# Two-stage agent attention with a routed expert: factors no longer normalised ahead of the split, and an explicit instruction order

## The chip, the cores and the metric

The kernel runs on one core of one Trainium2 chip. The metric is the device time of one execution in microseconds (us). The engines are PE (TensorE, matmuls; PEld is its weight load), DVE (VectorE), ACT (ScalarE), POOL (GpSimd) and SP (SyncE, which here issues nearly all DMA transfers).

## What is computed

For 4 batches of 12608 tokens with 128 channels and 49 agents, attention goes in two steps, and then a small expert corrects the 128 best tokens of each batch:

```python
def sm(a, b):
    s = scale * (a @ b.transpose(0, 2, 1))
    s = s - s.max(-1, keepdims=True)
    e = np.exp(s)
    return e / (e.sum(-1, keepdims=True) + 1e-09)
a2k = sm(agents, k)          # 49 x 12608
agent_v = a2k @ v            # 49 x 128
q2a = sm(q, agents)          # 12608 x 49
x = q2a @ agent_v
# expert: per batch, the 128 tokens with the largest x @ w_gate
h = np.maximum(x[top] @ w1, 0.0)
out[top] = x[top] + sigmoid(score[top])[:, None] * (h @ w2)
```

## The kernel before

**Tiling.** A batch is 99 columns of 128 tokens, in seven chunks: six of 15 columns (long, 960 KB a load) and chunk 6 of 9 (short, 576 KB). (b, c) is batch b, chunk c. k, q and v are loaded by chunk; tiles of loads and of finished outputs share the ring "inp" of 6 buffers (N_IN), and the batch-0 outputs that fill gaps (FILL) have a ring "og" of 2.

**The k side.** `scores` (k_front) multiplies a chunk with the agents on PE: tile S, in two halves, from a PSUM ring of 3. DVE transposes each half into sk and takes its maximum into mx. When all seven chunks are there, k_max makes the maxima of the batch (mT and mB on PE, then mb on DVE). k_exp subtracts mb on POOL and exponentiates on ACT. v_tiles multiplies with v on PE (av), and v_finish (pw and pp on PE, then DVE and ACT) makes ws, the values in two f16 parts, and iv, a power of two.

**The q side.** q_scores makes sq in the same way, with a maximum per token qm on DVE. q_exp subtracts qm on POOL and exponentiates on ACT; for batches in EARLY (0 and 1) DVE then sums, ACT adds a small constant, DVE takes the reciprocal, and q_high multiplies the factors with it on POOL. q_high copies the factors to f16 (ACT); q_low subtracts on POOL to get the low part; both stand in f. q_turn transposes f on PE (fT), ACT or DVE copies it to ft. q_gate makes gate scores and sums on PE (pg). q_rates, once all seven gates of a batch are there, makes the scores of the batch and, for batches not in EARLY, r, the reciprocal sum per token. topk (all, gt, pc and the rest) finds the 128 tokens.

**Outputs.** q_out multiplies ft and ws on PE, four columns at a time (po); an eviction writes og. MODES names the engine of each group of four: V is DVE, A is ACT, P is ACT with a POOL multiplication behind it. For EARLY batches the eviction scales with iv alone, for others with r (in V by DVE, in P by POOL). A chunk that is complete is stored by SP. At the end expert gathers the tokens (xq), multiplies (qT, sc, eT, xT, xe, ph, py on PE), and scatters its result once the stores of its batches have landed.

**The order.** All this is first recorded as a list of steps (Recorder; a step is one instruction or one group of matmuls), in program order and with dependencies. `place` then plays a model of the engines, with the priorities of the table RANKS, and returns the order in which the steps are issued; each engine works its part of it in order. PE has 452 steps in it, SP 118.

Of the kernel before, what the change touches and what calls it, by code (L numbers as in the profile page):

```python
# [40 lines left out]
EARLY = (0, 1)  # L41
MODES = ('AVAV', 'AVAV', 'VPVP', 'VPVP')
# [6 lines left out]
SLACK = 0.0  # L49
STICK = 10922.517314977244  # L50
# [202 lines left out]
HALF = ("po", "fT", "pg")  # L253
WINDOW, STAY, RISE = 3413.333, 0.45, 0.76
WORK = {"S": 1.0, "av": 0.89, "po": 0.93, "pg": 0.25, "fT": 0.8, "all": 0.83, "ph": 0.9}
RATE, GATHER, SCATTER = 408.0, 6500.0, 2400.0


def switch(a, b):

    if a in HALF and b in HALF:
        return 10.0
    return 160.0 if a == "av" else 100.0 if a == "S" or b in ("S", "av") else 50.0


def lag(a, b):

    if a.engine == b.engine:
        return 0.0 if a.engine == "PE" else a.tail
    return a.tail + 70.0  # L270


class Clock:


    def __init__(self):
        self.window, self.did, self.full = 0, 0.0, False

    def cost(self, op, t):
        while t >= (self.window + 1) * WINDOW:  # L280
            self.full = self.did >= (STAY if self.full else RISE) * WINDOW
            self.window, self.did = self.window + 1, 0.0
        few = op.kind == "pg"
        c = op.cost * (1.0 if self.full or few else 2.0)
        over = max(0.0, t + c - (self.window + 1) * WINDOW)
        self.did += (c - over) * WORK.get(op.kind, 0.5)
        if over:
            self.full = self.did >= (STAY if self.full else RISE) * WINDOW
            self.window, self.did = self.window + 1, over * WORK.get(op.kind, 0.5)
        return c  # L290


def place(rec, urgency, slack=0.0, stick=0.0):

    ops = rec.ops
    users, takes = {}, [[] for _ in ops]
    for op in ops:
        for name in sorted(op.uses):
            if name not in users:
                takes[op.seq].append(rec.rings[name][0])  # L300
            users.setdefault(name, []).append(op)
    rank = [(urgency(op.tag, op.engine), op.seq) for op in ops]
    room = {ring: bufs for ring, bufs in rec.rings.values()}
    left = {name: len(u) for name, u in users.items()}
    after = [[] for _ in ops]
    missing = [len(op.deps) for op in ops]
    for op in ops:
        for d in op.deps:
            after[d].append(op)
    ready = [0.0] * len(ops)  # L310
    queue = {e: [op for op in ops if op.engine == e and not op.deps] for e in ENGINES.values()}
    free = dict.fromkeys(queue, 0.0)
    last = dict.fromkeys(queue, "")
    times, ends, order = [0.0], [], []
    line, clock = 0.0, Clock()
    while len(order) < len(ops) or ends:
        if not times:
            raise RuntimeError("no instruction can begin")
        now = heapq.heappop(times)
        while ends and ends[0][0] <= now + 1e-6:  # L320
            op = ops[heapq.heappop(ends)[1]]
            for x in after[op.seq]:
                more = slack if x.engine == "PE" and op.engine != "PE" else 0.0
                ready[x.seq] = max(ready[x.seq], op.end + lag(op, x) + more)
                missing[x.seq] -= 1
                if not missing[x.seq]:
                    queue[x.engine].append(x)
                    heapq.heappush(times, ready[x.seq])
            for name in op.uses:
                left[name] -= 1  # L330
                if not left[name]:
                    room[rec.rings[name][0]] += 1
        for e, waiting in queue.items():
            if free[e] > now + 1e-6:
                continue
            best = None
            for op in waiting:
                if ready[op.seq] > now + 1e-6:
                    continue
                key = rank[op.seq]  # L340
                if op.kind == last[e]:
                    key = (key[0] - stick, key[1])
                if best is not None and key >= best[0]:
                    continue
                need = takes[op.seq]
                if all(room[r] >= need.count(r) for r in need):
                    best = (key, op)
            if best is None:
                continue
            op = best[1]  # L350
            waiting.remove(op)
            order.append(op)
            for r in takes[op.seq]:
                room[r] -= 1
            op.start = max(now, free["POOL"]) if op.two else now
            cost = op.cost
            if e == "PE":
                if last[e] != op.kind:
                    op.start += switch(last[e], op.kind) if last[e] else 50.0
                cost = clock.cost(op, op.start)  # L360
            last[e] = op.kind
            free[e] = op.end = op.start + cost
            if op.kind == "dma_start":
                line = max(line, op.start + 1800.0) + op.size / RATE
                op.end = line + 1700.0
            elif op.size:
                op.end += GATHER if op.label.startswith("xq") else SCATTER
            heapq.heappush(ends, (op.end, op.seq))
            heapq.heappush(times, op.end)
            heapq.heappush(times, free[e])  # L370
    return sorted(order, key=lambda op: (op.start, op.seq))


RANKS = {
    ('setup', 0): {"ACT": -7704.603, "POOL": -40854.573, "DVE": -34695.979},
# [9 lines left out]
    ('kmax', 0): {"DVE": 41091.545, "PE": 58712.794},  # L385
    ('exp', 0, 0): {"POOL": -88028.326, "ACT": 169482.5},
    ('exp', 0, 1): {"POOL": -22401.104, "ACT": 321716.736},
    ('exp', 0, 2): {"POOL": 70975.178, "ACT": 315931.785},
    ('exp', 0, 3): {"POOL": 58294.679, "ACT": 304754.866},
    ('exp', 0, 4): {"POOL": 39134.622, "ACT": 334237.156},  # L390
    ('exp', 0, 5): {"POOL": 51140.999, "ACT": 225861.786},
    ('exp', 0, 6): {"POOL": 55847.904, "ACT": 305110.098},
    ('v', 0, 0): {"SP": 11990.05},
    ('av', 0, 0): {"PE": 42293.51},
    ('v', 0, 1): {"SP": 20852.403},
    ('av', 0, 1): {"PE": -95203.721},
    ('v', 0, 2): {"SP": 25732.307},
    ('av', 0, 2): {"PE": 48113.417},
    ('v', 0, 3): {"SP": 26879.58},
    ('av', 0, 3): {"PE": 36554.066},  # L400
    ('v', 0, 4): {"SP": -154.989},
    ('av', 0, 4): {"PE": -244316.769},
    ('v', 0, 5): {"SP": 27655.575},
    ('av', 0, 5): {"PE": 87914.589},
    ('v', 0, 6): {"SP": 28400.238},
    ('av', 0, 6): {"PE": 38896.804},
    ('fin', 0): {"DVE": -136605.102, "PE": -175038.306, "POOL": 41207.367, "ACT": 135592.531},
    ('q', 0, 0): {"SP": -22705.261, "PE": 83217.232, "DVE": 73912.386},
    ('qe', 0, 0): {"POOL": 74676.234, "ACT": 353340.888, "DVE": 25400.62},
    ('turn', 0, 0): {"PE": 110425.037, "DVE": 86067.107, "ACT": 171382.578},  # L410
    ('gate', 0, 0): {"PE": 26353.217},
    ('q', 0, 1): {"SP": -23034.369, "PE": 53477.308, "DVE": -145606.484},
    ('qe', 0, 1): {"POOL": 82352.64, "ACT": 322967.816, "DVE": 37860.525},
    ('turn', 0, 1): {"PE": 83936.752, "DVE": 87178.494, "ACT": 316575.984},
# [228 lines left out]
    ('expert', 2): {"POOL": 38822.733, "PE": 214325.217, "DVE": -26426.609, "ACT": 335914.832},  # L643
    ('expert', 3): {"POOL": -240553.185, "PE": 107739.067, "DVE": -50621.084, "ACT": 308149.546},
}


def urgency(tag, engine):

# [864 lines left out]
```

## Time and profile before

| | us |
|---|---|
| median of 3 runs | 289.97 (289.36 to 291.24) |
| the profiled execution | 289.3 |
| its span | 287.4 |
| PE busy | 266.9 |
| DVE busy | 224.3 |
| POOL busy | 183.4 |
| ACT busy | 171.6 |
| moved by DMA | 106.68 MB |

Busy time is the time in which an engine executes something; matmuls are pipelined and their ends are modelled. A timeline row gives start and duration of merged instructions of one kind, with the idle time ahead of them and what ended it in brackets. A piece of the chain of waits lasts until the next piece of the chain begins. The granted clock of PE is given as a share of full speed.

### The profile page before, as it was taken

To read this page: it belongs to the slowest core of one execution; us is meant where nothing else is said; L and a number is where in the kernel's file an instruction comes from. 1 tells how busy PE (TensorE), PEld (TensorE's weight loads), DVE (VectorE), ACT (ScalarE), POOL (GpSimd) and SP (SyncE) were. 2 spreads that over 40 slices of the span, in tenths; PEclk is the share of its full clock that TensorE was granted. 3 is DMA by queue.
4 is the path that set the end of the run, shared out by engine and by line. 5 is a ranking of instruction groups with operands and counts; after the bars stand their busy time and mean duration, and the time that the engine had idled before them with its cause. 6 is when DMAs were issued, how large, how long until landed. Compare 5 with 4: busy or idle time off the path is not lost.

```text
span 287.4 us, 8559 instructions
## 1 busy us (share of the span) xinstructions
PE 266.9 (93%) x3524; PEld 176.3 (61%) x3524; DVE 224.3 (78%) x517; ACT 171.6 (60%) x313; POOL 183.4 (64%) x152
## 2 busy tenths in 40 slices
PE   1985798999999999999999999999999999999992
PEld 0221235594557645536455974656798789898992
DVE  1897897977999888997788979558925869998730
ACT  1004156553168965518496988979979854975500
POOL 8014799894189999119998329998422234784723
PEclk9999799999999999999999999889999999999997
DMA  7999999999999999999999999999813585999981
GB/s 281 424 408 419 422 426 415 422 417 422 418 421 391 380 423 410 408 421 412 418 423 419 421 422 414 413 420 373 320 52 148 222 349 220 414 413 408 419 372 48
DMA packets 18203, 106.68 MB, mean 371 GB/s; under 512 B 2032, under 2 KB 3440, under 8 KB 18160
## 3 DMA queue, kind: packets, MB, share of 16 engines
q1 hardware_dynamic: 17760, 105.42, 90.1%
q8 instruction: 30, 0.49, 0.7%
q0 software_dynamic: 256, 0.52, 0.5%
q10 hardware_dynamic: 144, 0.13, 0.1%
q14 instruction: 13, 0.11, 0.1%
HBM read 79.85 MB, written 26.21 MB: 369 GB/s over the span
## 4 chain that ended last, share of the span: by engine, by line
PE 65%; POOL 12%; DMA 9%; ACT 7%; DVE 3%; issue 3%; POOLq 0%; ACTq 0%
PE S L1435 24%; PE av L1435 13%; PE po L1435 13%; PE fT L1435 6%; POOL sk L1435 5%; DMA xT<-kT 4%; DMA out<-og 3%; POOL f L1435 3%; PE pg L1435 2%; PE all L1435 2%; ACT gt L1435 2%; PE ph L1435 2%; POOL sq L1435 2%; DMA ag_sb<-agT 2%; ACT ft L1435 2%
## 5 line engine op out<-in xcount | busy, mean ns | idle before, releaser
L1435 PE MATMUL S<-xT,ag_sb 128*32 128x480 f32 (+1 forms) x896 | 102.4, 572 | 10.8 <-DMA ag_sb<-agT 6.0
L1435 POOL TENSOR_TENSOR sq<-sq,qm 128x735 f32<-128x735 f32 (+1 forms) x42 | 56.9, 1368 | 34.9 <-DVE qm L1435 27.8
L1435 PEld LDWEIGHTS <-ft 128*128 128x128 f16 x1188 | 59.1, 98 | 15.1 <-issue 13.3
L1435 POOL TENSOR_TENSOR f<-sq,f 128x735 f16<-128x735 f32 (+1 forms) x28 | 42.7, 1527 | 23.5 <-ACT f L1435 21.2
L1435 PEld LDWEIGHTS S<-xT,ag_sb 128*32 128x32 f32 x896 | 23.5, 111 | 54.1 <-issue 24.6
L1435 PE MATMUL po<-ws,ft 128*128 128x128 f16 x792 | 53.5, 220 | 0.5 <-ACT og L1435 0.4
L1435 POOL TENSOR_TENSOR sk<-sk,mb 128x735 f32<-128x735 f32 (+1 forms) x28 | 47.2, 1703 | 8.8 <-DVE mb L1435 8.8
L1435 PE MATMUL av<-v,sk 128*64 128x129 f32 x792 | 49.9, 275 | 0.4 <-DMA v<-va 0.4
L1435 PEld LDWEIGHTS av<-v,sk 128*64 128x64 f32 x792 | 44.5, 136 | 8.5 <-DMA v<-va 3.6
L1435 ACT COPY ft<-fT 128x896 f16<-128x896 f16 (+2 forms) x49 | 43.7, 896 | 8.8 <-PE fT L1435 8.6
L1435 DVE STREAM_TRANSPOSE sq<-S 128x480 f32<-128x480 f32 (+1 forms) x56 | 35.5, 639 | 11.6 <-POOL f L1435 8.4
L1435 DVE STREAM_TRANSPOSE sk<-S 128x480 f32<-128x480 f32 (+1 forms) x56 | 35.1, 635 | 6.3 <-PE S L1435 3.5
L1435 DVE TENSOR_REDUCE qm<-sq 128x15 f32<-128x735 f32 (+1 forms) x42 | 36.1, 865 | 1.2 <-ACT sq L1435 0.7
L1435 ACT ACTIVATE sq<-sq,lift 128x735 f32<-128x735 f32 (+1 forms) x28 | 25.0, 891 | 19.5 <-POOL sq L1435 19.3
L1435 DVE TENSOR_REDUCE mx<-S 128x1 f32<-128x480 f32 (+1 forms) x56 | 33.0, 607 | 3.1 <-PE S L1435 2.9
L1435 POOL TENSOR_TENSOR og<-og,r 128x512 f32<-128x512 f32 (+1 forms) x26 | 24.3, 944 | 14.1 <-ACT og L1435 13.9
L1435 PEld LDWEIGHTS <-f 128*128 128x128 f16 x396 | 22.9, 98 | 12.2 <-issue 7.6
L1435 ACT ACTIVATE sk<-sk 128x735 f32<-128x735 f32 (+1 forms) x28 | 22.4, 799 | 12.4 <-POOL sk L1435 12.2
L1435 PE MATMUL fT<-idh,f 128*128 128x128 f16 x396 | 28.8, 220 | 0.8 <-POOL f L1435 0.8
L1435 ACT CAST f<-sq 128x735 f16<-128x735 f32 (+1 forms) x28 | 22.2, 793 | 11.1 <-POOL sq L1435 10.5
L1435 ACT ACTIVATE og<-po,iv 128x512 f32<-128x512 f32 (+1 forms) x28 | 18.0, 663 | 12.6 <-PE po L1435 11.5
L1435 DVE SCALAR_TENSOR_TENSOR gt<-all,top,minus 128x512 bf16<-128x512 f32 x32 | 23.6, 739 | 0.9 <-PE all L1435 0.5
(131 smaller groups left out, 251.2 us busy)
## 6 DMA issues: line engine op xcount, KB each, us to landing
v<-va SPq DMA_DIRECT2D x24, 967.5 KB, 8.8
xT<-kT SPq DMA_DIRECT2D x24, 960.0 KB, 9.1
xT<-qT SPq DMA_DIRECT2D x24, 960.0 KB, 9.0
out<-og SPq DMA_DIRECT2D x24, 960.0 KB, 6.4
v<-va SPq DMA_DIRECT2D x4, 580.5 KB, 6.9
xT<-kT SPq DMA_DIRECT2D x4, 576.0 KB, 8.8
xT<-qT SPq DMA_DIRECT2D x4, 576.0 KB, 9.1
out<-og SPq DMA_DIRECT2D x4, 576.0 KB, 5.6
```

The costliest lines, as they stand in the source:

```text
L1435: call(*args, **kwargs)
```

## The change

EARLY becomes empty, so no batch has its factors summed and scaled in q_exp and q_high; all four batches get r in q_rates, and all outputs are evicted in the modes V and P with r. The planner with its model, its prices and RANKS goes; `place` returns the steps in the order of a list of numbers, ORDER, each number being a step's place in the recorded program. The copies into f get their dependency on the two clearing memsets by name.

```diff
-EARLY = (0, 1)
-MODES = ('AVAV', 'AVAV', 'VPVP', 'VPVP')
+EARLY = ()
+MODES = ('VPVP', 'VPVP', 'VPVP', 'VPVP')
-SLACK = 0.0
-STICK = 10922.517314977244
...
-def place(rec, urgency, slack=0.0, stick=0.0):
...
-RANKS = {
...
+ORDER = (
+    10, 0, 3, 9, 221, 131, 224, 222, 223, 122, 225, 226, 6, 132, 133, 134, 135, 136, 227, 16, 15, 17, 18, 20,
...
+def place(rec):
+
+    order, done = [rec.ops[i] for i in ORDER], set()
+    for op in order:
+        assert op.deps <= done, op.label
+        done.add(op.seq)
+    assert len(done) == len(rec.ops)
+    return order
...
+    zeros = set()
     for i in range(N_F):
         f = qp.tile([P, TMAX, P], F16, tag="f", name=f"f0_{i}", bufs=N_F)
-        nc.gpsimd.memset(f, 0.0)
+        zeros.add(nc.gpsimd.memset(f, 0.0).seq)
...
-        copy(f[:, :n, :A], d["q", c][:, :n, :A])
+        copy(f[:, :n, :A], d["q", c][:, :n, :A]).deps.update(zeros)
...
-    order = place(rec, urgency, SLACK, STICK)
+    order = place(rec)
```

Counted through the recorded program (1466 steps before, 1444 after), the two orders read so. Loads at the start, before: k of batch 0 first (chunks 0, 4, 2, 5), then q 0.1, q 0.0, weights, k 0.6, 0.1, 0.3, q 0.3, v 0.4, k 1.0 and so on; after: q 0.6, q 0.0, k 0.0, q 0.5, k 0.6, k 0.3, q 0.3, k 0.1, q 0.1, q 1.0, k 0.4, k 0.5, k 0.2, q 1.3, q 0.2, k 1.0, v 0.0 and so on. The constants move from third to 32nd place, the expert's weights behind most loads.

Steps of PE in runs of one kind, before and after: S 49 and 46 runs, av 21 and 17, fT 38 and 42, po 48 and 56, pg 14 and 14. In the output stage the list before goes through chunks nearly one by one; the list after mixes them (around the first ph of the expert: 3.19, 2.27, 2.23, 3.19, 2.22, 2.21, 2.27). The last two stores are (2, 22) and (3, 14) before, (3, 17) and (3, 20) after, in the numbering of the tags (batch, running number).

## Rows read from the trace of the kernel before

**Rows 1.** The page: span, and busy time and share of PE.
```profile
span 287.4 us, 8559 instructions
PE 266.9 (93%) x3524; PEld 176.3 (61%) x3524; DVE 224.3 (78%) x517; ACT 171.6 (60%) x313; POOL 183.4 (64%) x152
```
**Rows 2.** Busy time by stretches: length, PE, PEld, DVE, ACT, POOL, clock, DMA share, GB/s.
```profile
10.00:20.00 10.00, 9.15 (x80) 2.10 (x72) 9.59 (x18) 0.00 (x0) 0.00 (x0) 1.00 1.02 412
...
180.00:190.00 10.00, 9.70 (x162) 5.68 (x154) 5.99 (x9) 9.06 (x12) 9.84 (x9) 0.83 1.04 417
...
210.00:220.00 10.00, 9.98 (x162) 9.08 (x158) 2.90 (x12) 8.14 (x17) 3.61 (x3) 1.00 0.25 102
```
**Rows 3.** Chain of waits, pieces on PE: start, time to the next piece, what.
```profile
63.16 0.94 PE fT L1435 x15
...
65.79 0.94 PE S L1435 x8
67.13 0.52 PE fT L1435 x8
67.64 1.75 PE S L1435 x16
...
73.57 1.11 PE S L1435 x16
...
84.86 1.91 PE av L1435 x30
...
88.80 3.45 PE av L1435 x60
```
**Rows 4.** PE's timeline at marks: start, duration, line, operation, operands, count, idle before.
```profile
47.25 1.98 PE L1435 MATMUL av<-v,sk 128*64 128x129 f32 x30 [0.41 <-DMA v<-va]
...
49.67 1.82 PE L1435 MATMUL S<-xT,ag_sb 128*32 128x480 f32 x16 [0.45 <-DMA xT<-qT]
51.99 1.01 PE L1435 MATMUL fT<-idh,f 128*128 128x128 f16 x15 [0.50 <-POOL f L1435]
...
66.67 0.46 PE L1435 MATMUL pw<-avs,cst 128*98 128x129 f32 x2
...
171.39 0.46 PE L1435 MATMUL pw<-avs,cst 128*98 128x129 f32 x2
...
186.34 1.83 PE L1435 MATMUL S<-xT,ag_sb 128*32 128x480 f32 x8
...
221.81 0.41 PE L1435 MATMUL pw<-avs,cst 128*98 128x129 f32 x2
...
281.56 0.39 PE L1435 MATMUL py<-w_end,hT 128*128 128x128 f32 x2
```
**Rows 5.** The page: GB/s moved in 40 equal slices of the span.
```profile
GB/s 281 424 408 419 422 426 415 422 417 422 418 421 391 380 423 410 408 421 412 418 423 419 421 422 414 413 420 373 320 52 148 222 349 220 414 413 408 419 372 48
```
**Rows 6.** Chain of waits, first and last of five pieces on POOL.
```profile
34.62 6.97 POOL sk L1435 x4
...
50.37 1.57 POOL f L1435
```
**Rows 7.** Instructions by form: operands, count, busy us, mean ns, idle time before.
```profile
L1435 POOL TENSOR_TENSOR sq<-sq,qm 128x735 f32<-128x735 f32 x36 | 51.4, 1440 | 33.1 <-DVE qm L1435 26.0 <-DVE iv L1435 7.0
...
L1435 DVE TENSOR_REDUCE qm<-sq 128x15 f32<-128x735 f32 x36 | 32.5, 909 | 0.9 <-ACT sq L1435 0.4
...
L1435 ACT ACTIVATE og<-po,iv 128x512 f32<-128x512 f32 x26 | 17.5, 686 | 12.6 <-PE po L1435 11.5 <-PE pc L1435 0.9 <-issue 0.2
L1435 DVE TENSOR_TENSOR og<-po,r 128x512 f32<-128x512 f32 x26 | 17.3, 685 | 1.5 <-PE po L1435 1.1
L1435 POOL TENSOR_TENSOR og<-og,r 128x512 f32<-128x512 f32 x14 | 14.6, 1042 | 11.5 <-ACT og L1435 11.3
...
L1435 ACT COPY og<-po 128x512 f32<-128x512 f32 x14 | 8.5, 608 | 2.0 <-PE po L1435 1.8
```
**Rows 8.** Chain of waits, its last transfer: start, time to the next piece.
```profile
273.07 9.32 DMA out<-og
```

More of the change, by code (lines that the diff above doesn't have):

```diff
@@ L250, in price @@
         op.two = op.two or two
[L253 to L270, printed above, removed]
@@ L273 @@
[L273 to L290, printed above, removed]
@@ L293, in place @@
-def place(rec, urgency, slack=0.0, stick=0.0):
[L295 to L371, printed above, removed]
@@ L648, in urgency @@
-def urgency(tag, engine):
-    return RANKS.get(tag, {}).get(engine, 0.0)
+ORDER = (
[73 rows of a table added]
+)
+def place(rec):
[5 more added lines that the diff above has]
+    return order
 def const_layout(capacity):
```

241 lines of the change are left out of this document (removed), and 102 rows, old and new, of tables (ORDER, RANKS).

## Prediction

> **What bounds the kernel now.** I read the page first, for the share of each engine and the span [rows 1]; then the busy time in stretches of 10 us [rows 2]: the reader is to see that PE is busy 9.98 of 10 us even in 210:220, where the DMA engines are at 0.25. A busy PE could still be a slow one, so I went on to the chain of waits for what a run of matmuls costs from its start to the next start [rows 3], and to PE's own timeline for where it stands at a given time [rows 4].
>
> From [rows 3]: half a score chunk (S, x8) takes 0.94 us alone, a second behind it 0.81, so entering S costs 0.13; a half of a short chunk (x16 in 1.11) 0.49. av costs 0.0513 per pass (3.45 less 1.91, over 30), 0.103 per token column, and 0.37 to enter. A transpose fT costs 0.06 (0.94 less 0.52, over 7), 0.05 to enter. Runs of po and pg follow the same way and are entered for almost nothing.
>
> With these prices I add up the PE work ahead of a mark and subtract it from the mark's time: the lead-in, by which PE is late against its own work. At the pw matmul of batch 0 (66.67): 33 long S halves (26.7), 4 short (2.0), 75 transposes (4.5), 99 av columns (10.2), 18 entries (3.1), two small ones (0.6), 47.1 in all; lead-in 19.6. At pw of batch 2 (171.39) the same sum gives 151.7: 19.6 again. So between 66 and 171 us PE loses nothing: the time is lead-in, plus PE work (262.9 us for all 452 PE steps), plus an end. After 184 it loses 1.6: S x8 takes 1.83 in place of 0.94 at 186.34, and the stretch has a granted clock of 0.83 [rows 2, 4]; at pw of batch 3 (221.81) the lead-in is 21.2. PE ends at 281.95; the sum overprices the last 60 us by 2.1, in both kernels alike.
>
> What makes the 19.6? Two things that end together. The loads: a long chunk is 0.983 MB and moves in 2.37 us at 414 GB/s, the mean of the saturated slices [rows 5], a short one in 1.42. PE waited for v chunk (0, 1) until 47.25 and for q chunk (0, 5) until 49.67 [rows 4]; the loads up to these add up to 42.9 and 45.3, so data is usable 4.4 us after that sum. v chunk (0, 2) (20 long loads, 2 short, 1.2 us of constants and weights: 51.4) is usable at 55.8, with 36.0 us of PE work ahead: 19.8. And POOL: from the column maxima of batch 0 on it stands on the chain from 34.6 to 51.9 [rows 6], and PE's fT at 51.99, with 32.4 us of work ahead, waits for it [rows 4]: 19.6.
>
> **The change, part by part.**
>
> EARLY empty, removed: 14 POOL multiplications (the 1.44 us row holds the subtraction and this one; the short ones less): 19 us. 14 DVE sums at 0.91 or less: 12 us; with each a small reciprocal and a small ACT step [rows 7].
>
> EARLY empty, added: per batch 0 and 1 four small DVE steps and one ACT step over 99 columns, estimated at 2 us from the 0.91 of 735 columns. 26 POOL multiplications of outputs at 1.04 (four tokens) or less: 24 us. 26 ACT copies at 0.61 take the place of 28 scaling evictions at 0.69: ACT 3 us less. DVE evicts 28 groups in place of 26, about 1 us [rows 7]. Sum: POOL +5, DVE -9 or better, ACT less, PE 0. None is on the path between 66 and 171, since PE covers all three there; without that cover POOL's 5 would be the loss. On the path lie only the multiplications of batch 0 before 52 us: without them POOL's half of the lead-in falls, and the loads' 19.8 stays. Taken alone this part gives nothing.
>
> A new wait: outputs of batches 0 and 1 need r, hence all seven gates of their batch. The list puts one po of batch 0 ahead of these gates; its bank is the one only fill outputs use, and the next po there comes 31 us of PE work later. On DVE score transposes of batch 1 stand behind r, and PE would wait for those; but their matmuls stand behind the gates too. I price it at 0, at most the 3 us that the gates take.
>
> The list, lead-in: eight of the first fifteen loads are q chunks, and k of batch 0 is complete with the 13th. A q chunk gives PE 1.75 of scores and 0.94 of transposes per 2.37 us of DMA, a k chunk 1.75 alone until the maxima exist. So PE has more to do early. I looked for the load with the largest (usable less work ahead): k chunk (2, 0), the 36th DMA on the queue. 30 long (71.1), 4 short (5.7), constants 0.9: 77.7, usable at 82.0. Work ahead: 46 long halves 37.3, 6 short 2.9, 137 transposes 8.2, 99 av columns 10.2, 36 entries 5.0, six small ones 1.9: 65.5. Lead-in 16.5. The other engines ask for less. DVE must put 14 transposes and 14 maxima of k, 13 transposes and 6 maxima of q through before the maxima of batch 0: 35 us by the page's means, where it did 29 us of such work before POOL's start at 34.6; so near 40. Then POOL subtracts, 1.74 [rows 6], ACT exponentiates, under 1, and av of chunk 0 can start at 43, with 31.4 us of work ahead: 11.6. POOL's later steps ask for 9 or less. So 16.5 stands, a gain of 3.1; its bounds are 15.5 (all slices at 426 GB/s) and 19.6.
>
> The list, PE entries: av is entered 17 times, not 21 (-1.5), S 46, not 49 (-0.4), fT 42, not 38 (+0.2), po 56, not 48 (+0.1): -1.5 after rounding. The 1.6 after 184: nothing in the list tells whether it comes back; from 0 to 1.6, and I keep it.
>
> The list, end: PE ends at 281.95 - 3.1 - 1.5 = 277.3, and PE's path takes 5.4 more, 282.8. Behind the last po stand 9.0 us of expert matmuls; so the last po ends near 268.3, copy and POOL multiplication take it to 270.3. The last store landed 9.3 us after its issue in the kernel before, with others ahead of it, 5.0 before the end [rows 8]; with the same backlog it lands at 279.6 here, end 284.6. I take 283, between the two. The profiled execution has 1.9 around its span of 287.4 and lies 0.7 below the median of the runs: 283 + 2.6 = 285.5.
>
> **Rivals.**
>
> *Given back at the end.* Six buffers serve the output tiles; a chunk can open when the store six back has landed. By the same sums the chunks of the new list open 0 to 5 us after that, those of the old 3.7 or more, since the new list keeps more chunks open at once; 39 outputs there pass POOL, not 26. The last store landed at 282.4, 4.4 later than such sums have it. Then 4 us come back: 289, the same. Against it: DMA has slack, 102 GB/s in 210:220 [rows 2].
>
> *The clock.* S x8 at 1.83 [rows 4] shows what a small wait can bring: half clock, 1.6 us with what follows. The start of the new list has gaps too: fT of the first q chunk needs DVE, POOL, ACT and POOL again, with only 6 us of PE work ahead of it. Three such falls make 290, two 288.7. [...]
>
> *Slower: the maxima of batch 0.* They come near 40 by my sum, not 34. Seven subtractions, exponentials, av, fin, gates and r of batch 0 queue behind them in a fixed order. The lead-in of this path is 11.6 and grows 1:1 with the delay. It decides once the maxima come after 48; at 53.5 (DVE waits in order for scores whose load is late) the lead-in is 25 and the time 294. For it: DVE was busy 9.59 of 10 us in 10:20 [rows 2]. Against: 8 us of margin.
>
> *The list does not help the start.* If loads fall behind early, because a k tile is held over several q chunks and only five buffers turn, the lead-in is 19 again, and only the entries count: 288.
>
> **How the numbers follow.** Forecast 285.5, chance 0.58; its own range is 282 to 288 (lead-in 15.5 to 18, with and without the 1.6, store backlog). Given back at the end 0.14, clock 0.09, no help at the start 0.07, slower path 0.12. About 1% (287.1 and 292.9) is what a measurement here can tell from no change. Faster: 0.55 of the forecast and 0.05 of the first two rivals. Slower: 0.12 and 0.01 of the clock. Same: the other 0.27. The range 281 to 291 leaves out 0.06 below and 0.13 above.
>
> **What would show it.** Right: on PE's timeline pw of batch 0 (61.1 us of work ahead) near 77.6 and k chunk (2, 0) near 82; PE's waits for kT loads up to there; stores landing 6 to 9 us after issue. Wrong: the maxima copied after 48 us; half clock before 40 us; PE's po after 235 us waiting for evictions whose tiles wait for stores; POOL's og multiplications on the chain's end for more than 10 us.

## The result, and the profile after

The changed kernel takes 292.61 us in the median of 18 runs (290.39 to 294.03); the kernel before, on the same chips, 290.07 (288.61 to 293.52). The ratio is 1.0082, 95% interval 1.0057 to 1.0106. So the change makes the kernel slower by just under 1%; the forecast was 285.5, range 281 to 291. The profiled execution took 292.55 us, 2.25 of them around its span.

The page of the changed kernel, span and busy times, then the granted clock of PE in 40 slices of 7.26 us (tenths; 9 is 90% or more):

```profile
span 290.3 us, 8556 instructions
PE 264.8 (91%) x3524; PEld 176.7 (61%) x3524; DVE 218.2 (75%) x497; ACT 166.2 (57%) x299; POOL 188.4 (65%) x164
...
PEclk9999999997899999999999999999999999999999
```

Against [rows 1], PE is busy 2.1 less, DVE 6.1 less, POOL 5.0 more: POOL as the prediction summed it, PE near it (1.5), DVE 3 short of it, of which one constant made at a bad moment is 2.0 (tri_i, below). What did not come out is when PE works. Its timeline between 57 and 90 us (start, duration, operation, operands, count, idle time before and what ended it):

```profile
59.08 1.01 PE L1122 MATMUL fT<-idh,f 128*128 128x128 f16 x15
60.02 2.62 PE L1122 MATMUL S<-xT,ag_sb 128*32 128x480 f32 x24
62.57 3.58 PE L1122 MATMUL av<-v,sk 128*64 128x129 f32 x60
70.59 1.01 PE L1122 MATMUL fT<-idh,f 128*128 128x128 f16 x8 [4.44 <-ACT ft L1122]
71.53 4.70 PE L1122 MATMUL S<-xT,ag_sb 128*32 128x288 f32 x32
...
82.30 0.46 PE L1122 MATMUL pw<-avs,cst 128*98 128x129 f32 x2
...
87.11 1.01 PE L1122 MATMUL S<-xT,ag_sb 128*32 128x480 f32 x8
```

At 66.15 PE has nothing that it may begin: its next step in the order, the transposes of q chunk (0, 4), waits 4.44 us for ACT. Behind this wait 32 score matmuls take 4.70 us, where the price of the prediction is 2.73 (two long halves, two short ones and the entry). The last row is k chunk (2, 0), the load that the forecast took for the limit: it was to start at 82.0 with 65.5 us of work ahead; it starts at 87.11, a lead-in of 21.6 in place of 16.5. Up to av at 62.57 the same sum gives 14.7; so the jump lies between 66 and 76 us, and it is 6.9: the wait of 4.44, 0.4 for the 8 transposes (0.94 to the next start, priced 0.53), and 2.0 for the scores.

What ACT did in that time, what POOL did, and one copy on DVE:

```profile
62.32 0.84 ACT L1122 ACTIVATE sk<-sk 128x735 f32<-128x735 f32 x1
65.16 0.58 ACT L1122 ACTIVATE sk<-sk 128x441 f32<-128x441 f32 x1 [2.00 <-POOL sk L1122]
66.56 0.92 ACT L1122 ACTIVATE sq<-sq,lift 128x735 f32<-128x735 f32 x1 [0.82 <-POOL sq L1122]
67.51 0.82 ACT L1122 CAST f<-sq 128x735 f16<-128x735 f32 x1
68.23 1.53 ACT L1122 ACTIVATE sk<-sk 128x735 f32<-128x735 f32 x2
69.66 0.88 ACT L1122 COPY ft<-fT 128x896 f16<-128x896 f16 x1
```
```profile
62.42 1.61 POOL L1122 TENSOR_TENSOR f<-sq,f 128x735 f16<-128x735 f32 x1
63.98 1.14 POOL L1122 TENSOR_TENSOR sk<-sk,mb 128x441 f32<-128x441 f32 x1
65.08 1.44 POOL L1122 TENSOR_TENSOR sq<-sq,qm 128x735 f32<-128x735 f32 x1
66.47 1.78 POOL L1122 TENSOR_TENSOR sk<-sk,mb 128x735 f32<-128x735 f32 x1
```
```profile
63.28 0.68 DVE L1122 COPY ft<-fT 128x1024 f16<-128x1024 f16 x1
```

The copy at 69.66 empties the buffer (in PSUM, the memory that takes PE's results) that holds the last 7 columns of q chunk (0, 2), transposed by PE at 59.08 to 60.09. It needs nothing from POOL. But in ACT's fixed order it stands behind the exponentials of k chunks 6, 4 and 5 and the exponential and f copy of q chunk (1, 1), and these wait for POOL, which has worked since 55.8 with gaps of less than 0.2 us. ACT is idle for 2.8 of the 4 us from 63 to 67 while the copy could run. There are two buffers for transposes, taken in turn; so PE stops. The other one is no help: it holds the first 8 columns of the chunk, DVE empties it at 63.28 to 63.96, but in this list the last 7 columns are transposed ahead of the first 8, so the buffer that waits for ACT is the one whose turn it is.

A second jump, 2.0, comes at 102 to 105. PE, DVE and POOL there:

```profile
104.99 1.42 PE L1122 MATMUL S<-xT,ag_sb 128*32 128x480 f32 x12 [1.79 <-DVE sq L1122]
```
```profile
100.01 2.27 DVE L1122 TENSOR_TENSOR tri_i<-cst,idf 128x128 bf16<-128x128 f32 x1
```
```profile
94.34 6.40 POOL L1122 TENSOR_TENSOR sk<-sk,mb 128x735 f32<-128x735 f32 x4
100.70 1.43 POOL L1122 TENSOR_TENSOR sq<-sq,qm 128x735 f32<-128x735 f32 x1
```

tri_i, a constant made once, took 0.28 us in the kernel before, when POOL was idle:

```profile
9.16 0.28 DVE L1435 TENSOR_TENSOR tri_i<-cst,idf 128x128 bf16<-128x128 f32 x1
```

Here it ends 0.15 after POOL's last instruction. A third jump, 1.8 us at 161 to 166, is mostly PE waiting for q loads (0.38, 0.51) and for an ft copy (0.51), 1.4 in all. PE's end, and what stood behind the last row of [rows 4]:

```profile
284.81 0.39 PE L1122 MATMUL py<-w_end,hT 128*128 128x128 f32 x2
```

PE ends at 285.20, 3.25 later than before, with 1.4 us less work by the sum (261.5); 5.1 us follow, 5.4 before.

### The profile page after: what moved, and what is told of

It is laid out like the page before. It is cut to its first block, busy times and chain, and to the rows that moved or that the text cites. A ratio compares the mean times of both kernels' runs of the same rounds, so it can differ in the third digit from the quotient of the medians.

```text
span 290.3 us, 8556 instructions
## 1 busy us (share of the span) xinstructions
PE 264.8 (91%) x3524; PEld 176.7 (61%) x3524; DVE 218.2 (75%) x497; ACT 166.2 (57%) x299; POOL 188.4 (65%) x164
## 4 chain that ended last, share of the span: by engine, by line
PE 40%; POOL 21%; DVE 15%; issue 9%; ACT 8%; DMA 6%; POOLq 0%; DVEq 0%
PE S L1122 12%; PE po L1122 10%; POOL sk L1122 8%; POOL sq L1122 6%; PE av L1122 5%; POOL f L1122 5%; DMA xT<-qT 4%; PE fT L1122 3%; PE py L1122 3%; PE ph L1122 2%; ACT gt L1122 2%; DVE sq L1122 2%; DVE og L1122 2%; DVE mx L1122 2%; ACT sq L1122 2%
## 5 line engine op out<-in xcount | busy, mean ns | idle before, releaser
L1122 PE MATMUL S<-xT,ag_sb 128*32 128x480 f32 (+1 forms) x896 | 101.2, 571 | 12.5 <-DMA ag_sb<-agT 5.4
L1122 POOL TENSOR_TENSOR sq<-sq,qm 128x735 f32<-128x735 f32 (+1 forms) x28 | 38.2, 1364 | 31.3 <-DVE qm L1122 23.3
L1122 POOL TENSOR_TENSOR og<-og,r 128x512 f32<-128x512 f32 (+1 forms) x52 | 48.0, 941 | 11.2 <-ACT og L1122 10.2
L1122 PE MATMUL po<-ws,ft 128*128 128x128 f16 x792 | 54.4, 219 | 0.6 <-DVE og L1122 0.2
L1122 ACT COPY ft<-fT 128x896 f16<-128x896 f16 (+2 forms) x49 | 42.7, 898 | 12.6 <-PE fT L1122 12.5
L1122 PE MATMUL av<-v,sk 128*64 128x129 f32 x792 | 48.4, 275 | 0.6 <-ACT sk L1122 0.6
L1122 DVE TENSOR_TENSOR og<-po,r 128x512 f32<-128x512 f32 (+1 forms) x56 | 35.6, 654 | 11.8 <-PE po L1122 10.6
L1122 ACT COPY og<-po 128x512 f32<-128x512 f32 (+1 forms) x52 | 27.0, 536 | 16.9 <-PE po L1122 14.1
L1122 PE MATMUL fT<-idh,f 128*128 128x128 f16 x396 | 29.9, 221 | 5.8 <-ACT ft L1122 5.2
L1122 DVE SCALAR_TENSOR_TENSOR gt<-all,top,minus 128x512 bf16<-128x512 f32 x32 | 23.7, 741 | 2.0 <-PE all L1122 1.4
L1122 DVE TENSOR_REDUCE qm<-sq 128x15 f32<-128x735 f32 (+1 forms) x28 | 24.1, 865 | 0.6
```

Of the source, the lines that this page charges most:

```text
L1122: call(*args, **kwargs)
```

## The experiments

Ratios are to the kernel before, run beside each experiment.

**The copy ahead of the queue.** One number of the list moves; 84 is the exponential of k chunk 6, 174 the copy. Five ACT steps stand between the two places (the text below counts a sixth, the exponential of chunk 3, behind which the copy stays).

```diff
-  ... 201, 300, 83, 84, ... 80, ... 81, 82, 103, 104, 174, 332, ...
+  ... 201, 300, 83, 174, 84, ... 80, ... 81, 82, 103, 104, 332, ...
```

> One step of the list is moved: the ACT copy that empties the second half of q chunk (0, 2)'s transposes (7 columns) goes ahead of the exponential of the short k chunk 6 of batch 0, so that it stands no longer behind six ACT steps that wait for POOL. Theory (a copy queued behind exponentials): the transposes of q chunk (0, 4), which waited 4.44 us for this copy, start near 66.2 in place of 70.6 us; the half clock of 70 to 76 us does not appear (granted clock above 0.95 from 60 to 80 us); pw of batch 0 comes at 76.5 to 78.5 in place of 82.3 us; the tri_i stall at 102 stays, so the time is 286.5 to 289. Rival 1 (the maxima of batch 0 are late and POOL's backlog sets the pace): PE waits as long at av of chunks 4 and 5 for their exponentials, pw stays at 81 or later, time 291 to 293. Rival 2 (loads): pw is early, but PE waits for loads instead and its lead-in is back at 21 us by 100, time 291 to 293.

Measured: 286.99 us (286.64 to 287.07), ratio 0.988, interval 0.983 to 0.993; again on another chip, in six executions:

> The first run's kernel again in five rounds on the same chip: 286.6 to 287.3. If the triangles by ACT are worth something (lead-in of 16.7 in place of 17.9 at 110 us in the profiled executions), the seventh run's kernel is 0.5 to 1.2 us faster than this one; if the loads at 155 us take it back, the two are equal within 0.3.

286.63 (286.40 to 287.68), 0.9876 (0.9834 to 0.9918). ACT, then PE, of this kernel:

```profile
62.01 0.84 ACT L1120 ACTIVATE sk<-sk 128x735 f32<-128x735 f32 x1
62.74 0.88 ACT L1120 COPY ft<-fT 128x896 f16<-128x896 f16 x1
64.86 0.58 ACT L1120 ACTIVATE sk<-sk 128x441 f32<-128x441 f32 x1 [1.24 <-POOL sk L1120]
```
```profile
65.79 0.62 PE L1120 MATMUL fT<-idh,f 128*128 128x128 f16 x8
66.34 3.10 PE L1120 MATMUL S<-xT,ag_sb 128*32 128x288 f32 x32
69.97 0.85 PE L1120 MATMUL av<-v,sk 128*64 128x129 f32 x10 [0.53 <-DMA v<-va]
...
75.81 0.46 PE L1120 MATMUL pw<-avs,cst 128*98 128x129 f32 x2
76.77 1.82 PE L1120 MATMUL S<-xT,ag_sb 128*32 128x480 f32 x16 [0.49 <-DMA xT<-qT]
79.22 1.82 PE L1120 MATMUL S<-xT,ag_sb 128*32 128x480 f32 x16 [0.32 <-DMA xT<-kT]
81.65 1.01 PE L1120 MATMUL S<-xT,ag_sb 128*32 128x480 f32 x8
...
279.14 0.39 PE L1120 MATMUL py<-w_end,hT 128*128 128x128 f32 x2
```

The wait is gone, the scores behind it run at 3.10, and PE waits for nothing but loads: v, q, k. k chunk (2, 0) starts at 81.65, forecast 82.0, a lead-in of 16.15, forecast 16.5. Neither rival holds: av doesn't wait for exponentials, and PE ends 5.67 earlier than in the changed kernel, so nothing was given back. This one place in ACT's order costs 5.6 us, all of the loss of 2.5 and 3.1 more.

**A dose between.** The same copy between the exponential (416) and the f copy (417) of q chunk (1, 1), so still behind two of the five.

> A dose between the changed kernel and the first experiment: the same ACT copy is put ahead of the f copy of q chunk (1, 1), so behind three of the six ACT steps that wait for POOL. Theory (PE's transposes of q chunk (0, 4) begin when this copy ends, 1 to 1): the copy ends near 68.4, the transposes wait 1.8 to 2.4 us in place of 4.44 and none; pw of batch 0 near 77.7 to 78.5 without a fall of the clock, up to 80 with one; time 288.5 to 290.5, between 286.99 and 292.61. Rival (a threshold: nothing is lost unless the clock falls): time 287 with a wait of 2 us.

289.41 us (287.89 to 290.97), ratio 0.9944 (0.990 to 0.9989). ACT and PE:

```profile
66.37 0.92 ACT L1120 ACTIVATE sq<-sq,lift 128x735 f32<-128x735 f32 x1 [0.81 <-POOL sq L1120]
67.19 0.88 ACT L1120 COPY ft<-fT 128x896 f16<-128x896 f16 x1
```
```profile
68.13 1.01 PE L1120 MATMUL fT<-idh,f 128*128 128x128 f16 x8 [2.16 <-ACT ft L1120]
69.07 3.99 PE L1120 MATMUL S<-xT,ag_sb 128*32 128x288 f32 x32
```

The copy ends at 68.07, the transposes start at 68.13; in the changed kernel 70.54 and 70.59. So 1 to 1. The half clock comes with the wait: the scores take 3.10 with none, 3.99 behind 2.16 us, 4.70 behind 4.44. Read us by us, the granted clock is 0.50, the lower of PE's two levels (1.2 GHz), from 69 to 75 in the changed kernel and from 69 to 71 here, and 1.00 (2.4 GHz) from 60 to 80 in the first experiment. The Trainium skill, "TensorE: Matmul & The Clock Gate", section "HAM oscillation — how this bites in real kernels", says of a kernel whose PE waits long for data that its clock falls in the wait and the next burst starts cold; the two rows with a wait agree. No run takes the wait away and leaves the half clock; by the prices the clock's part of the jump is 2.4 of 6.9. Whether anything is lost without such a fall (the rival of the expectation), the profiled execution can't tell, since the clock fell in it. But two of the ten executions have a mean granted clock of 0.996 and 1.000, and they took 287.89 and 287.99 us, 1 us more than the first experiment (286.99, its clock 0.996): as far as two executions show it, the wait costs time by itself.

**tri_i from one tensor.**

```diff
-    nc.vector.tensor_tensor(tri_i, cs("tri"), idf, op=ALU.add)
+    nc.vector.tensor_scalar(tri_i, cs("srow")[:, :P], cs("pcol"), None, op0=ALU.is_gt)
```

> The list is that of the changed kernel; only tri_i (a constant triangle with its diagonal) is made in another way at the same place: a comparison of one row of constants with a number per partition, in place of the sum of two tensors in SBUF. Theory (a DVE instruction that reads two tensors from SBUF stands still while POOL works without a gap): it takes 0.2 to 0.35 us in place of 2.27, PE's wait of 1.79 us for sq at 105 goes, and the time falls by 1 to 2 us, 290.6 to 291.6. Rival (it is the place, for instance the constants that land late): it still takes about 2.2 us and the time stays at 292.6. Third possibility: the stall goes, but a later wait takes the same back, time 292 to 293.

292.16 us (291.13 to 293.69), ratio 1.0059 (1.0027 to 1.0091): by the time, no difference from the changed kernel. DVE and POOL:

```profile
100.38 0.71 DVE L1120 TENSOR_SCALAR tri_i<-cst 128x128 bf16<-128x128 f32 x1
```
```profile
99.57 1.44 POOL L1120 TENSOR_TENSOR sq<-sq,qm 128x735 f32<-128x735 f32 x1
```

My theory (DVE waits when it reads two tensors from SBUF, the on-chip memory of the tiles that are not in PSUM) falls as the whole account: this form reads one tensor and still ends with POOL, 101.09 and 101.01; it is shorter only because POOL was nearer its end. PE's wait at 105 is gone, but in this execution 24 score matmuls at 90.50 took 4.25 in place of 2.62, without a wait ahead; more on that below. So what the stall costs in time is not shown.

**tri_i by a reduction** over a length of one, a form that is not of the kinds which waited so far:

```diff
+    t0 = spot["tri"][0] + 1
+    nc.vector.tensor_reduce(tri_i, cst[:, t0:t0 + P].unsqueeze(2), axis=AX.X, op=ALU.max)
```

> The list of the changed kernel; tri_i is made at the same place by a DVE reduction over a length of one, which reads one tensor from SBUF, as the maxima per token do (0.92 us in the middle of POOL's gap-free work, the same as elsewhere). The comparison in the second run also read one tensor and still ended only with POOL's work (0.71 us, POOL's end at 101.01, its own at 101.09). Theory now (only some forms of DVE instruction wait for POOL's instruction to end, a copy to bf16 and a sum of two SBUF tensors among them, not a reduction): tri_i takes 0.2 to 0.35 us though POOL is at work. Rival (all DVE instructions that read these constants at this place wait for POOL): it ends within 0.2 us of the end of a POOL instruction again, 0.5 to 2.3 us long. The time is one look, near 291 to 292.

```profile
100.91 0.28 DVE L1121 TENSOR_REDUCE tri_i<-cst 128x128 bf16<-128x128 f32 x1
```
```profile
100.03 1.46 POOL L1121 TENSOR_TENSOR sq<-sq,qm 128x735 f32<-128x735 f32 x1
```

0.28 in the middle of POOL's instruction, at the same place, from the same constants: it is the form, not the place. A single execution took 292.38, with the scores behind the gates at 4.30: no gain shown here either. The Trainium skill names the mechanism: "SBUF — State Buffer", section "SBUF: two separate sides", has DVE and GpSimd share a pair of ports under an exclusive lock, which DVE needs with two SBUF inputs or in a two-port mode; "Advanced Engine Details and Errata", section "VectorE Performance Modes", gives such a mode to casts and tensor_scalar and none to reductions. All three forms measured here agree.

**Both together** (the copy in front, tri_i from one tensor), and then the copy with both triangles made by ACT:

> Both edits: the copy of q chunk (0, 2) ahead of the queued exponentials, and tri_i from one tensor. Theory: the two losses add up, 4.4 with the half clock's 2.3 at 66 to 76 us and 2.0 at 102 us, less what the loads then ask for (the lead-in that the loads allow was put at 16.5); time 284.5 to 287.5, faster than the kernel before by 1 to 2 per cent. Rival (the lead-in is set by loads and by buffers that come free too late): lead-in of 21 or more by 110 us again, time 289 to 292.

287.26 us (286.56 to 287.36), 0.9885 (0.9834 to 0.9937): the two do not add up. With the copy in front POOL is 6 us earlier, and tri_i in its old form takes only 0.54 in the first experiment and 0.29 in its repeat, so there was little to win. There it is tri_b, a cast, that hangs: 1.26 us at 88.74, and PE waits 0.78 for sq behind it.

```diff
-    nc.vector.tensor_copy(tri_b, cs("tri"))
+    nc.scalar.copy(tri_b, cs("tri"))
...
+    nc.scalar.copy(tri_i, cst[:, t0:t0 + P])
```

> The copy of q chunk (0, 2) ahead of the queued exponentials, and both triangles of constants made by ACT copies in place of DVE steps. Theory (DVE's copy, 1.26 us at 88.74, and PE's wait of 0.78 for sq behind it come from POOL's work; ACT does not wait for POOL): the two copies take 0.2 to 0.35 each, PE's wait at 90.6 goes, lead-in at 108 is 17.0 or less in place of 17.9; time 286.0 to 286.9. Rival (the next wait takes it back, loads at 156 above all): 287 as before.

> The seventh run's kernel again in five rounds, on the chip of the ninth, to compare with it and with the first: 286 to 288 with a spread of 2.5, if the clock falls in some executions and not in others; the ratio to the kernel before 0.985 to 0.991.

286.95 (285.82 to 288.32) and 286.19 us (285.39 to 287.51); ratios 0.9858 (0.978 to 0.9935) and 0.9867 (0.9821 to 0.9912). The ACT copies take 0.28 each, and the lead-in at 110 us falls to 16.7 by the same sum (17.9 in the first experiment). Against the first experiment on the same chip it is 0.44 faster in the median, less than its own spread of 2.1; that it is faster is not shown. Both kernels beat the one before, by 1.2 to 1.4%.

**The gates split.** In five profiled executions (the experiments above with 4.25 to 4.32, and 4.06 in the repeat of the first) the scores right behind the gates of batch 0 ran at half clock, in four others, the changed kernel's among them, they took 2.62. Here, in the kernel with both triangles by ACT, 546, the second half of scores of k chunk (2, 0), moves between the gates.

```diff
-  ... 145, 235, 545, 175, 569, 340, 566, 420, 205, 160, 421, 190, 220, ... 244, 546, ...
+  ... 145, 235, 545, 175, 569, 340, 566, 420, 546, 205, 160, 421, 190, 220, ... 244, ...
```

> The seventh run's kernel (copy first, triangles by ACT) with one more move: PE's second half of scores of k chunk (2, 0), which stood behind the gates of batch 0, is put between the third and the fourth of these seven gates. In four profiled runs (the second, third, sixth and eighth) the scores right behind the gates ran at half clock, x24 in 4.25 to 4.32 us in place of 2.62, though PE had not waited: 99 gate matmuls of 3 columns and 15 transposes came before; in the others they didn't. Theory (the stretch of small gate matmuls is near what lets the clock fall, and whether it falls differs from one execution to the next): with the scores between them no run of this kernel falls there; the times lie close together, 285.8 to 286.5, median about 0.7 below the seventh run's kernel. Rival (the fall has another cause, or r of batch 0, 0.9 us later, costs the same): no difference, or the same spread of 285.8 to 288.3.

287.30 us (286.77 to 287.60), 0.9891 (0.985 to 0.9932), where the kernel without this move took 286.19 beside it: not 0.7 faster, as expected, but 1.1 slower. PE of this kernel, and the same scores in the repeat of the first experiment:

```profile
87.47 1.82 PE L1121 MATMUL S<-xT,ag_sb 128*32 128x480 f32 x16
90.77 1.01 PE L1121 MATMUL S<-xT,ag_sb 128*32 128x480 f32 x8 [1.48 <-DVE sq L1121]
```
```profile
85.25 0.94 PE L1120 MATMUL pg<-ws,ft 128*128 128x3 f16 x30
86.12 4.06 PE L1120 MATMUL S<-xT,ag_sb 128*32 128x480 f32 x24
```

The scores run at full clock. The mean granted clock of each execution says more: in the ten executions of the kernel without the move (its two runs), five at 0.995 to 1.000 took 285.39 to 286.25 us and five at 0.992 to 0.994 took 286.87 to 288.32; with the move all six are at 0.995 to 1.000. So the clock does vary between executions of one kernel, and with the move the low values are gone. The smaller spread, 0.83 us, says little by itself: the four executions of the first experiment, with the gates in one stretch, lie within 0.43. But r of batch 0 comes 1.1 later, DVE's transposes of q chunk (1, 4) stand behind it, and PE waits 1.48 for them: what the clock gave, this wait took. With six runs and one profile, that the stretch of gates lets the clock fall is likely and not settled.

**The other half of the change by itself.** No batch in the early set, modes V and P, but the steps in the order of the kernel before. Steps that fall away are left out, new ones stand where those that they replace stood; what this half costs holds for these places.

> The other half of the change by itself: no batch in the early set, modes V and P, but the steps stand in the order of the kernel before (steps that fall away are left out, new ones stand where the old ones that they replace stood, the four reciprocal steps of a batch at the place of its raw scores; one fill output that now needs r moves behind it). Theory of the prediction (this half gives nothing: loads hold the lead-in at 19.6 and PE covers POOL's extra 5 us): 288.5 to 291.5. Rival 1 (it is a loss, hidden in the changed kernel: waits for r or POOL's multiplications on the path): 292 or more. Rival 2 (it is a gain, since POOL is free of 14 multiplications at the start): 286 to 288. The run of the rates with the planner, 321.93 us, would then be the planner's order and not the rates.

302.34 us (301.60 to 303.17), ratio 1.0375 (1.0296 to 1.0453). PE's order is that of the kernel before but for one output; pw of batch 0 comes at 66.73 (66.67 before), pw of batch 2 at 176.32 (171.39) and pw of batch 3 at 232.45 (221.81). So 4.9 of the 12 us are lost by 176 and 5.7 up to 232. In the first part PE waits at the matmuls `all` of batches 0 and 1 for DVE's top, which now stands behind the steps of r; before, it did not wait there:

```profile
83.24 1.13 PE L1120 MATMUL all<-idf,top 128*128 128x128 f32 x8 [1.23 <-DVE top L1120]
...
163.36 2.34 PE L1120 MATMUL all<-idf,top 128*128 128x128 f32 x16 [1.12 <-DVE top L1120]
```

The busy times from 175 to 210 us of the kernel before, of this one and of the changed one (length, PE, PEld, DVE, ACT, POOL, clock, DMA share, GB/s), and this one's transposes by line:

```profile
175.00:210.00 35.00, 34.49 (x499) 23.06 (x498) 25.84 (x58) 31.50 (x52) 28.47 (x21) 0.95 0.97 377
```
```profile
175.00:210.00 35.00, 30.17 (x419) 18.87 (x416) 20.91 (x53) 23.88 (x41) 31.94 (x25) 0.95 0.92 346
```
```profile
175.00:210.00 35.00, 34.13 (x497) 22.30 (x495) 24.59 (x52) 28.96 (x43) 34.37 (x29) 1.00 1.01 403
```
```profile
L1120 PE MATMUL fT<-idh,f 128*128 128x128 f16 x396 | 29.1, 221 | 5.0 <-POOL f L1120 4.2 <-ACT ft L1120 0.7
```

In this stretch POOL is busy 31.94 of 35 us, and five multiplications of outputs (4.8 us) stand among its f steps; PE's transposes wait 4.2 us for f in the whole kernel. The changed kernel's list asks more of POOL in this stretch (34.37 of 35) and PE keeps working: it has other work ready. So the list is what makes this half of the change bearable. That POOL's queue and the steps of r are the causes is read from these rows, and the waits shown make up only part of the 12 us; no run took the multiplications or the steps of r alone away.

With the planner of before in place of its order:

> The kernel before with its own planner and priorities, and only the other part of the change: no batch in the early set, modes V and P for all outputs. The prediction says that this part alone gives nothing: 289 to 291, POOL 5 us busier, DVE 6 to 9 us less. Rival (POOL's extra multiplications or the wait for r are on the path): 292 or more. Second rival (POOL's 14 multiplications out of the start are worth something by themselves): 286 to 288.

317.32 to 323.79 us in four executions; the ratio of 1.098 (1.0887 to 1.1073) is that of the two faster ones (317.32 and 320.29). That is another 16 us, which the planner with its table of priorities, made for the other steps, adds; what in it does so was not looked into.

## Why the prediction was wrong

**What held.** The sums: POOL +5.0 (5), DVE -6.1 (9 or better), PE work -1.4 (-1.5). The maxima of batch 0: 42.4 (near 40), and av of chunk 0 at 45.52 (43), early enough:

```profile
42.39 0.21 DVE L1122 COPY mb<-mB 128x49 f32<-128x49 f32 x1 [0.96 <-PE mB L1122]
```
```profile
45.52 1.97 PE L1122 MATMUL av<-v,sk 128*64 128x129 f32 x30
```

The lead-in of the loads: 16.15 in the first experiment (16.5), where PE waits for v, q and k from 70 to 82 us, as written under "what would show it". The end: 5.1 us behind PE (5.7), so nothing was given back there.

**The step that failed** is "The other engines ask for less ... POOL's later steps ask for 9 or less". I set POOL's steps against the PE steps that use their results, and took ACT for free since it is busy 60% of the time. I didn't go through ACT's order. A copy that needs only PE stood there behind five steps that need POOL, at a time when POOL had a backlog; and PE needed its buffer. In the sum it is the lead-in, 16.5 in the forecast and 21.6 measured. Price in time: 5.6 us. It turned a gain of 3 us into a loss of 2.5.

**The second term** is what PE loses after the start. I kept the 1.6 at 184 and added nothing. From k chunk (2, 0) to the end of PE the lead-in went from 19.6 to 19.05 before (281.95 less 262.9), and from 21.6 to 23.7 after (285.20 less 261.5): 2.65 more. In the first experiment it is 16.15 to 18.0, 2.4 more, which is why that kernel takes 287 and not 285.5. With the 5.1 us of the lead-in, the 2.65 are nearly all of the 7.9 by which PE ended later in the changed kernel than forecast (285.20, 277.3). In the changed kernel the larger parts, by PE's rows, are tri_i's stall, 2.0, and the q loads and the ft copy at 161 to 166, 1.8; the loss at 184 did not come back at its place. I had written that the constants move from the third to the 32nd load and never asked which instructions follow them into POOL's busy time.

**"Taken alone this part gives nothing"** is wrong by 12 us in the order of the kernel before. The sentence that PE covers POOL's 5 us was worked out from 66 to 171 us only; after that POOL already had 28.47 of 35 us to do in the kernel before. And the wait for r, priced at 0, came in another place than the one that I looked at: 1.23 and 1.12 us at `all`, inside the stretch that I took as covered.

**The rivals.** *The clock* was right in kind: half clock behind a wait, here one fall, not three, and with the wait as the larger part.

Its example, the scores at 1.83 in the kernel before, need not be the work of a small wait. There is one of 0.30 us ahead of them, but also 69 gate matmuls and 15 transposes, and behind such a stretch the clock fell in other runs without any wait (last section):

```profile
182.11 1.98 PE L1435 MATMUL pg<-ws,ft 128*128 128x3 f16 x69
...
184.81 0.75 PE L1435 MATMUL fT<-idh,f 128*128 128x128 f16 x8 [0.30 <-POOL f L1435]
```

*Slower* named the delay of batch 0's maxima past 48 us; they came at 42.4, so its condition was not met, though its place (POOL's backlog behind the maxima, steps queued in a fixed order) is where the loss arose. *Given back at the end* and *the list does not help the start* are refuted by PE's end and by 16.15.

## What to carry to other kernels

In a fixed order, follow each engine's own sequence: a cheap step that frees a buffer must not stand behind steps that wait for a backlogged engine, however idle its engine is on average. For each buffer ring with few buffers, look for the step that empties it and for what stands ahead of that step. Where a list moves an instruction out of an idle stretch, ask what else works beside it at the new place.

## What was not expected of the hardware

A DVE cast, comparison or sum of SBUF tensors of 128 x 128 takes 0.21 to 0.29 us when POOL is idle; begun while POOL works, it ended 0.08 to 0.16 us after a POOL instruction did and took up to 2.27. It can also miss a change between two POOL instructions: the one of 2.27 us began at 100.01, POOL's fourth subtraction gave way to the next at 100.70, and it ended behind that one, at 102.28. Reductions with an SBUF input go on at their usual times: qm at 95.65, beside POOL's subtractions, 0.92, mean 0.909 [rows 7].

The granted clock fell in some executions and not in others of the same kernel at the same place, behind 99 gate matmuls of 3 columns each and 15 transposes, with no wait ahead: 24 score matmuls took 2.62 us in one profiled execution of the first experiment's kernel and 4.06 in another.
